# Turning k' over 128 rows and projecting v onto the diagonals of a zeroed bank in a Linformer-attention and SwiGLU kernel

## The chip, the cores and the metric

The kernel runs on one core of one Trainium2 chip. The metric is the device time of one execution in microseconds (us). The **span** of a trace is shorter than that by about 1.7 us (569.4 for an execution of 571.14): it goes from the first to the last instruction.

## The reference

```python
k_proj = einsum('ks,bhsd->bhkd', E, k)              # 8 batches, 8 heads, 1024 tokens, 64 deep
v_proj = einsum('ks,bhsd->bhkd', F, v)              # k and v are shortened to 64 rows a head
attn   = softmax(q @ k_proj.T / 8)                  # 1024 x 64 per head
x      = (attn @ v_proj).transpose(0, 2, 1, 3).reshape(8192, 512)
out    = (silu(x @ w_gate) * (x @ w_val)) @ w_out   # w_gate, w_val 512 x 1536; w_out 1536 x 512
```

Inputs and output are fp32. The kernel computes in bf16 with fp32 sums.

## The kernel before

The gated network takes most of TensorE's time. It goes through 16 chunks of 512 tokens, two a batch, and for each of 12 blocks of 128 features makes one group of four matmuls for the gate (`gps`) and one for the value (`vps`). Two such groups of a block are followed by part of an output (`yps`). Between the groups lie numbered **slots**, in which the attention of the next chunk or batch is placed, piece by piece. Batches are numbered from 0 in the code and here; "second batch" at a timeline near 55 us is batch 1. Batch 0 can hide behind nothing: its attention is the start of the program, and the first two blocks are worked in two token halves, each as soon as its x is there.

The projection of k and v, and the turning of the projected k (k'), before the change:

```python
def u_KV(b, what="kv", hs=(0, H), at="a"):
    ...
    for j in range(NJ):                                  # k to rows 0-63 of the bank, v to rows 64-127
        for _, lo, w, src in todo:
            nc.tensor.matmul(out=t[lo:lo+64, h0:h1]..., lhsT=w[:, j, :], rhs=src[b][:, h0:h1, j, :], ...)
    if "k" in what:                                      # ks has 64 partitions
        nc.scalar.copy(out=kvp[b, "s"][:, h0:h1], in_=t[0:64, h0:h1])
    if "v" in what:                                      # even heads to one diagonal block, odd to the other
        eng = nc.vector if b else nc.scalar
        copy(eng, BDV[b % 2][0:64, ps, 0:64], tv[:, ps, 0, :])
        copy(eng, BDV[b % 2][64:128, ps, 64:128], tv[:, ps, 1, :])

def u_KT(b, at="a", prs=(0, NPAIR)):
    t = bank(at, [P, NPAIR, KP], BF16, "kTp")
    for pr in range(*prs):                               # 64 rows x 128 columns, turned to 128 x 64
        nc.tensor.transpose(out=t[:, pr, :], in_=ks[:, 2*pr:2*pr+2, :]..., identity=ident_bf[:KP, :KP])
    ...                                                  # VectorE copies kTp into the diagonals of BD
```

`BD` and `BDV` hold k' and v' of two heads on the diagonal of a 128x128 tile, so that one matmul serves two heads. The order of the start, after the fourth set of scores:

```python
u_KV(0, "v", (0, 4), at="y"); warm(1); u_KV(0, "v", (4, 6), at="y")
u_PV2(0, 0, 0, 0, act);       u_A(0, 2, dve)             # attention product; turning of attention weights
u_KV(0, "v", (6, 8), at="y"); u_A(0, 1, act)
u_PV2(0, 0, 1, 0, act);       u_A(0, 3, dve);  u_PV2(0, 0, 0, 1, dve)
load_w_gv(4, 6);  load_q(0, 1);  load_w_gv(6, 8) ...     # one queue, in this order
```

Batches 1 to 7 get their transposed q (`qTd`) by a transposing transfer on SyncE's queue (`u_TD`).

The softmax here doesn't subtract the row's maximum and nothing guards it: scores larger than these inputs give would overflow.

## Time and profile before

| what | us | from |
|---|---|---|
| time, median of 3 executions | 571.42 (571.02 to 571.66) | results |
| lost at changes of form, 47.5 us to the end | 3.39, of this 1.53 at k' | starts of TensorE's groups, less their regular spacing |
| TensorE's waits for weights of blocks 6 and 7 | 0.76 | the same |
| TensorE's wait for x of the second chunk | 0.47 | the same |
| slack of batch 2's first transposed q | 0.46 | landing at 104.58, first scores at 105.04 |

The sum of the busy time cannot show the losses at the changes of form. This is the windows view of the kernel before (from:to, length, then busy us and instructions of each engine, granted clock, DMA share in units of one engine's time, GB/s):

```profile
core 0: us, PE busy (x) PEld busy (x) DVE busy (x) ACT busy (x) POOL busy (x), PEclk, DMA share, GB/s
47.50:569.00 521.50, 518.43 (x2637) 241.04 (x2635) 304.32 (x514) 209.97 (x364) 79.47 (x80) 1.00 0.57 103
```

TensorE seems idle for 521.50 - 518.43 = 3.07 us. But an end of a matmul is modelled, and the length that the profile gives a matmul runs on into a drain. The losses are read from starts alone: group start to group start, less the number of matmuls times their spacing (0.216 us for 512 columns, 0.056 for 128, about 0.03 for 64).

### The profile page before, as it was taken

The numbers are of one execution on the slowest core, as the hardware profiler recorded it, in microseconds if no ns is written. First come the engines' busy times: TensorE is split into PE (matmuls) and PEld (weight loads), VectorE is DVE, ScalarE is ACT, GpSimd is POOL, SyncE is SP. The second block draws the span as 40 slices with busy tenths as digits, with TensorE's granted clock in tenths as the row PEclk, the third lists the DMA queues.
The fourth block names the chain that finished last, engine by engine and source line by source line (L and its number), as shares of the span: only waits on it lengthen the run. The fifth ranks groups of instructions, "written<-read, shape, count | busy, mean of one in ns | idle before, by whom it ended". The sixth has DMA issues, their size and how long they took to land.

```text
span 569.4 us, 7879 instructions
## 1 busy us (share of the span) xinstructions
PE 562.6 (99%) x2939; PEld 266.7 (47%) x2939; DVE 335.2 (59%) x577; ACT 236.8 (42%) x417; POOL 109.1 (19%) x122
## 2 busy tenths in 40 slices
PE   8999999999999999999999999999999999999997
PEld 5654444444444444444444444444444444444444
DVE  4776664766476655666466655666546665545550
ACT  4565442454435433443435434354343543443222
POOL 6742250124002400124002230023100220000000
PEclk9999999999999999999999999999999999999999
DMA  9999979829903696039931399105990213010002
GB/s 211 179 199 198 167 131 201 141 60 205 198 18 75 108 177 141 37 56 158 189 79 38 75 178 207 41 20 104 191 185 20 57 38 75 37 38 37 20 37 94
DMA packets 111143, 62.91 MB, mean 110 GB/s; under 512 B 64256, under 2 KB 102400, under 8 KB 111104
## 3 DMA queue, kind: packets, MB, share of 16 engines
q0 software_dynamic: 42800, 29.36, 36.3%
q1 hardware_dynamic: 67392, 31.46, 25.6%
q10 hardware_dynamic: 912, 1.57, 0.9%
q8 instruction: 23, 0.38, 0.3%
q14 instruction: 16, 0.13, 0.1%
HBM read 60.29 MB, written 16.78 MB: 135 GB/s over the span
## 4 chain that ended last, share of the span: by engine, by line
PE 92%; DMA 3%; DVE 2%; POOL 1%; ACT 1%; issue 0%; ACTq 0%; DVEq 0%; POOLq 0%
PE yps L362 29%; PE vps L324 28%; PE gps L324 27%; PE kvp L149 3%; PE sc L229 2%; PE pv L287 2%; DMA wv<-in_moe_w_val_dram 2%; DMA kraw<-in_k_dram 1%; DVE zz L244 1%; POOL AA L260 0%; POOL wg L117 0%; DVE hT L348 0%; ACT xT L137 0%; DVE s L343 0%; PE kTp L174 0%
## 5 line engine op out<-in xcount | busy, mean ns | idle before, releaser
L343 DVE SCALAR_TENSOR_TENSOR s<-th,gps 128x512 f32<-128x512 f32 x192 | 130.5, 679 | 143.1 <-ACT th L336 143.0
L324 PE MATMUL gps<-xT,wg 128*128 128x512 bf16 (+1 forms) x776 | 197.8, 377 | 0.6 <-DMA wg<-in_moe_w_gate_dram 0.4
L324 PE MATMUL vps<-xT,wv 128*128 128x512 bf16 (+1 forms) x776 | 197.5, 377 | 0.1
L362 PE MATMUL yps<-wo,hT 128*128 128x512 bf16 (+1 forms) x780 | 194.5, 376 | 0.0
L336 ACT ACTIVATE th<-gps 128x512 f32<-128x512 f32 x192 | 114.6, 597 | 157.9 <-PE gps L324 156.4
L348 DVE TENSOR_TENSOR hT<-s,vps 128x512 bf16<-128x512 f32 x192 | 132.0, 688 | 20.0
L260 POOL TENSOR_TENSOR AAd<-ee,rr 128x512 bf16<-128x512 f32 x56 | 58.3, 1041 | 343.3 <-issue 157.2
L362 PEld LDWEIGHTS <-hT 128*128 128x128 bf16 x780 | 76.2, 98 | 89.9
L324 PEld LDWEIGHTS <-wv 128*128 128x128 bf16 x776 | 73.9, 98 | 83.9 <-issue 3.3
L324 PEld LDWEIGHTS <-wg 128*128 128x128 bf16 x776 | 73.9, 98 | 82.1 <-issue 1.0
L372 ACT ACTIVATE ysb<-yps 128x512 f32<-128x512 f32 (+1 forms) x65 | 38.4, 591 | 76.7 <-PE yps L362 76.7
L137 ACT CAST xT<-pv 128x512 bf16<-128x512 f32 x63 | 36.6, 585 | 51.0 <-PE pv L287 50.1
L244 DVE TENSOR_REDUCE zz<-ee 128x8 f32<-128x512 f32 x64 | 43.4, 679 | 21.8 <-ACT ee L233 21.8
L233 ACT ACTIVATE ee<-sc 128x512 f32<-128x512 f32 x64 | 37.9, 595 | 23.6 <-PE sc L229 22.3
L229 PEld LDWEIGHTS <-qTd 128*128 128x128 bf16 x224 | 17.2, 98 | 13.2
L287 PE MATMUL pv<-AT,BDV 128*128 128x512 bf16 x60 | 22.4, 379 | 0.0
L229 PE MATMUL sc<-BD,qTd 128*128 128x128 bf16 x224 | 21.6, 219 | 0.0
L137 DVE CAST BDV<-kvp 64x256 bf16<-64x256 f32 x14 | 6.0, 426 | 20.0 <-ACT ks L159 17.8
L246 DVE RECIPROCAL rr<-zz 128x8 f32<-128x8 f32 x64 | 13.0, 203 | 7.4 <-DVE zz L244 1.4
L149 PE MATMUL kvp<-vb,FT 128*64 128x512 bf16 (+2 forms) x80 | 15.6, 338 | 0.3 <-ACT BDV L137 0.3
L149 PE MATMUL kvp<-kb,ET 128*64 128x512 bf16 (+1 forms) x72 | 15.5, 357 | 0.5 <-DMA kb<-in_k_dram 0.3
L107 POOL DMA_DIRECT2D qb<-in_q_dram x17 | 15.6, 919 | 0.6 <-DMA wv<-in_moe_w_val_dram 0.6
(51 smaller groups left out, 126.3 us busy)
## 6 DMA issues: line engine op xcount, KB each, us to landing
out_dram<-ysb SPq DMA_DIRECT2D x63, 256.0 KB, 2.4
qb<-in_q_dram POOLq DMA_DIRECT2D x15, 512.0 KB, 18.2
kb<-in_k_dram POOLq DMA_DIRECT2D x7, 1024.0 KB, 11.0
vb<-in_v_dram POOLq DMA_DIRECT2D x7, 1024.0 KB, 14.4
wo<-in_moe_w_out_dram POOLq DMA_DIRECT2D x2, 768.0 KB, 21.8
wg<-in_moe_w_gate_dram POOLq DMA_DIRECT2D x5, 256.0 KB, 9.5
wv<-in_moe_w_val_dram POOLq DMA_DIRECT2D x5, 256.0 KB, 10.1
kraw<-in_k_dram ACTq DMA_DIRECT2D x2, 512.0 KB, 4.7
```

Of the source, the lines that this page charges most:

```text
L137: (nc.scalar.copy if eng is nc.scalar else eng.tensor_copy)(out=out, in_=in_)
L149: nc.tensor.matmul(out=t[lo : lo + 64, h0:h1].rearrange("p h d -> p (h d)"), lhsT=w[:, j, :], rhs=src[b][:, h0:h1, j, :], start=(j == 0), ...
L229: nc.tensor.matmul(out=ps[:, n, :], lhsT=t[:, n, :], rhs=BD[b % 2][:, 4 * g + n, :], start=True, stop=True)
L233: nc.scalar.activation(out=e[:].rearrange("p h j k -> p (h j k)"), in_=ps[:].rearrange("p a k -> p (a k)"), func=AF.Exp, scale=scale,)
L244: nc.vector.reduce_sum(out=z[:], in_=e[:], axis=AX.X)
L260: eng.tensor_tensor(out=a.rearrange("p j h k -> p h j k"), in0=ee.pop((b, u))[:], in1=rr.pop((b, u))[:].unsqueeze(3).to_broadcast([P, 4, 2 ...
L324: nc.tensor.matmul(out=ps[:, ts], lhsT=(wg, wv)[w][:, kt, f * P : (f + 1) * P], rhs=x[:, kt, ts], start=(kt == 0), stop=(kt == NKT - 1),)
L336: nc.scalar.activation(out=th[:], in_=ps[:], func=AF.Tanh, scale=0.5)
L343: nc.vector.scalar_tensor_tensor(out=s1[:], in0=th[:], scalar=1.0, in1=g[:], op0=ALU.add, op1=ALU.mult)
L348: nc.vector.tensor_tensor(out=hT[c][:, f, :], in0=s1[:], in1=ps[:], op=ALU.mult)
L362: nc.tensor.matmul(out=yy[c][:, cs], lhsT=hT[c][:, f, i * P : (i + 1) * P], rhs=wo[:, f, cs], start=(f == 0), stop=(f == NFT - 1),)
L372: nc.scalar.activation(out=ysb[:, cs], in_=yy[c][:, cs], func=AF.Copy, scale=0.5)
```

## The change

It has four parts. **k'**: turned over all 128 rows (the lower 64 zero), to have the form of the matmuls beside it. **v of the first batch**: projected straight onto the diagonals of a bank that one matmul of zeros has cleared, so that one copy takes a piece out instead of two; the order of the start is rearranged with it. **q of the second chunk**: loaded in head halves, so that the weights of blocks 6 and 7 come ahead of its second half. **Slots**: the second chunk's attention one slot earlier, its last copies on two engines.

```diff
+    ks = [const.tile([P, H, D], BF16, name=f"ks{i}") for i in range(2)]     # rows 64-127 set to 0
...
+            nc.scalar.copy(out=ks[b % 2][0:64, h0:h1], in_=t[0:64, h0:h1])
...
+    def u_V0(p0, p1, at):
+        t = bank(at, [P, p1 - p0, P], FP32, "kvp")
+        nc.tensor.matmul(out=t[:]..., lhsT=zeros[:, 0:P], rhs=zeros[:, 0 : (p1 - p0) * P], start=True, stop=False)
+        src = vb[0][:].rearrange("p (a c) j d -> p a c j d", c=2)
+        for j in range(NJ):
+            for c in range(2):
+                nc.tensor.matmul(
+                    out=t[64 * c : 64 * c + 64, :, 64 * c : 64 * c + 64],
+                    lhsT=FT[:, j, :], rhs=src[:, p0:p1, c, j, :], start=False, stop=(j == NJ - 1))
+        nc.scalar.copy(out=BDV[0][:, p0:p1, :], in_=t[:])
...
-        t = bank(at, [P, NPAIR, KP], BF16, "kTp")
+        t = bank(at, [P, NPAIR, KP], FP32, "kTp")
-            nc.tensor.transpose(out=t[:, pr, :], in_=ks[...], identity=ident_bf[:KP, :KP])
+            nc.tensor.matmul(out=t[:, pr, :], lhsT=ks[b % 2][...], rhs=ident_bf[:, 0:KP], start=True, stop=True)
...
-        for i in range(2): ... nc.vector.memset(BDV[i][:], 0.0)
+        nc.vector.memset(BDV[1][:], 0.0)                                     # and two memsets of ks[i][64:P]
...  (order of the start)
+        u_V0(0, 2, "y");  u_PV2(0, 0, 0, 0, act);  warm(1);  u_V0(2, 3, "y");  u_A(0, 2, dve)
+        u_PV1(0, 0, 2, 0, dve)
+        u_V0(3, 4, "v");  u_PV1(0, 0, 3, 0, act);  u_N(0, 3)
+        f_mm(0, 0, 0, 0); u_A(0, 1, act);  u_A(0, 3, dve);  f_mm(0, 0, 1, 0)
+        u_PV2(0, 0, 0, 1, act);  u_PV2(0, 0, 1, 1, dve);  f_mm(0, 1, 0, 0);  f_mm(0, 1, 1, 0)
...
-        load_q(0, 1)
+        load_q(0, 1, hs=(0, 4));  load_w_gv(6, 8);  load_q(0, 1, hs=(4, 8));  load_w_gv(8, 10) ...
...
-            put(12 + i, u_T, 0, u);  put(14 + i, u_S, 0, u);  ...  put(19 + i, u_A, 0, u, nc.scalar)
+            put(11 + i, u_T, 0, u);  put(13 + i, u_S, 0, u);  ...  put((17, 18, 20, 21)[i], u_A, 0, u, nc.scalar)
-        put(21, u_PV, 0, 1, 0);  put(22, ...);  put(23, u_PV, 0, 1, 2);  put(23, u_PV, 0, 1, 3)
+        put(19, u_PV, 0, 1, 0);  put(20, ...);  put(22, u_PV, 0, 1, 2);  put(22, u_PV, 0, 1, 3, nc.vector)
```

More of the change, by code (lines that the diff above doesn't have):

```diff
@@ L101, in load_v, with load_q @@
             )
-    def load_q(b, ch, js=(0, 4)):
-        if js[0] == 0:
+    def load_q(b, ch, js=(0, 4), hs=(0, H)):
+        if js[0] == 0 and hs[0] == 0:
             qb[b, ch] = q_pool.tile([P, H, 4, D], BF16, name="qb", tag="qb")
-        js = slice(*js)
+        js, hs = slice(*js), slice(*hs)
         nc.gpsimd.dma_start(
-            out=qb[b, ch][:, :, js, :].rearrange("p h j d -> p h (j d)"),
-            in_=q[b].rearrange("h (p c j) d -> p c h j d", c=2, j=4)[:, ch, :, js, :].rearrange(
+            out=qb[b, ch][:, hs, js, :].rearrange("p h j d -> p h (j d)"),
+            in_=q[b, hs].rearrange("h (p c j) d -> p c h j d", c=2, j=4)[:, ch, :, js, :].rearrange(
                 "p h j d -> p h (j d)"
@@ L156, in u_KV @@
         if "k" in what:
-            if (b, "s") not in kvp:
-                kvp[b, "s"] = aw.tile([KP, H, D], BF16, name="ks", tag="ks")
-            nc.scalar.copy(out=kvp[b, "s"][:, h0:h1], in_=t[0:64, h0:h1])
+            nc.scalar.copy(out=ks[b % 2][0:64, h0:h1], in_=t[0:64, h0:h1])
         if "v" in what:
@@ L162, in u_KV @@
             ps = slice(h0 // 2, h1 // 2)
-            eng = nc.vector if b else nc.scalar
-            copy(eng, BDV[b % 2][0:64, ps, 0:64], tv[:, ps, 0, :])
-            copy(eng, BDV[b % 2][64:128, ps, 64:128], tv[:, ps, 1, :])
+            nc.vector.tensor_copy(out=BDV[b % 2][0:64, ps, 0:64], in_=tv[:, ps, 0, :])
+            nc.vector.tensor_copy(out=BDV[b % 2][64:128, ps, 64:128], in_=tv[:, ps, 1, :])
         if h1 == H:
             kvp.pop(key)
+    def u_V0(p0, p1, at):
+        t = bank(at, [P, p1 - p0, P], FP32, "kvp")
+        nc.tensor.matmul(
+            out=t[:].rearrange("p a d -> p (a d)"),
+            lhsT=zeros[:, 0:P], rhs=zeros[:, 0 : (p1 - p0) * P],
+            start=True, stop=False,
+        )
+        src = vb[0][:].rearrange("p (a c) j d -> p a c j d", c=2)
+        for j in range(NJ):
+            for c in range(2):
+                nc.tensor.matmul(
+                    out=t[64 * c : 64 * c + 64, :, 64 * c : 64 * c + 64],
+                    lhsT=FT[:, j, :],
+                    rhs=src[:, p0:p1, c, j, :],
+                    start=False,
+                    stop=(j == NJ - 1),
+                )
+        nc.scalar.copy(out=BDV[0][:, p0:p1, :], in_=t[:])
     def u_KT(b, at="a", prs=(0, NPAIR)):
-        ks = kvp[b, "s"]
-        t = bank(at, [P, NPAIR, KP], BF16, "kTp")
+        t = bank(at, [P, NPAIR, KP], FP32, "kTp")
         for pr in range(*prs):
-            nc.tensor.transpose(
+            nc.tensor.matmul(
                 out=t[:, pr, :],
-                in_=ks[:, 2 * pr : 2 * pr + 2, :].rearrange("p h d -> p (h d)"),
-                identity=ident_bf[:KP, :KP],
+                lhsT=ks[b % 2][:, 2 * pr : 2 * pr + 2, :].rearrange("p h d -> p (h d)"),
+                rhs=ident_bf[:, 0:KP],
+                start=True,
+                stop=True,
             )
@@ L309, in u_PV2, with u_PV1 @@
         copy(eng, xT[b, ch][:, 2 * g : 2 * g + 2, 256 * i : 256 * (i + 1)], ps[:])
+    def u_PV1(b, ch, pr, i, eng):
+        ps = ps_a.tile([P, CW // 2], FP32, name="pv", tag="pa")
+        nc.tensor.matmul(
+            out=ps[:].rearrange("p (j t) -> p j t", t=P),
+            lhsT=BDV[b % 2][:, pr, :],
+            rhs=AT[b, ch][:, 2 * i : 2 * i + 2, pr, :],
+            start=True,
+            stop=True,
+        )
+        copy(eng, xT[b, ch][:, pr, 256 * i : 256 * (i + 1)], ps[:])
     gp = {}
@@ L443 @@
         for i in range(2):
+            nc.vector.memset(ks[i][64:P], 0.0)
             nc.vector.memset(BD[i][:], 0.0)
-            nc.vector.memset(BDV[i][:], 0.0)
+        nc.vector.memset(BDV[1][:], 0.0)
         def turn(which, at, halves=(0, 1)):
@@ L512 @@
         u_R(0, 3)
-        u_N(0, 3)
-        u_KV(0, "v", (0, 4), at="y")
-        warm(1)
-        u_KV(0, "v", (4, 6), at="y")
-        u_PV2(0, 0, 0, 0, act)
-        u_A(0, 2, dve)
-        u_KV(0, "v", (6, 8), at="y")
+        u_V0(0, 2, "y")
+        u_PV2(0, 0, 0, 0, act)
+        warm(1)
+        u_V0(2, 3, "y")
+        u_A(0, 2, dve)
+        u_PV1(0, 0, 2, 0, dve)
+        u_V0(3, 4, "v")
+        u_PV1(0, 0, 3, 0, act)
+        u_N(0, 3)
+        f_mm(0, 0, 0, 0)
         u_A(0, 1, act)
-        u_PV2(0, 0, 1, 0, act)
         u_A(0, 3, dve)
-        u_PV2(0, 0, 0, 1, dve)
-        load_w_gv(4, 6)
-        load_q(0, 1)
-        for f in (6, 8, 10):
-            load_w_gv(f, f + 2)
+        f_mm(0, 0, 1, 0)
+        u_PV2(0, 0, 0, 1, act)
+        u_PV2(0, 0, 1, 1, dve)
+        f_mm(0, 1, 0, 0)
+        f_mm(0, 1, 1, 0)
+        load_w_gv(4, 6)
+        load_q(0, 1, hs=(0, 4))
+        load_w_gv(6, 8)
+        load_q(0, 1, hs=(4, 8))
+        load_w_gv(8, 10)
+        load_w_gv(10, 12)
         load_q(1, 0)
@@ L531 @@
         load_wo(1)
-        f_mm(0, 0, 0, 0)
-        u_PV2(0, 0, 1, 1, act)
-        f_mm(0, 0, 1, 0)
-        f_mm(0, 1, 0, 0)
-        f_mm(0, 1, 1, 0)
-        for i, u in enumerate(range(4, 8)):
-            put(12 + i, u_T, 0, u)
-            put(14 + i, u_S, 0, u)
-            put(15 + i, u_R, 0, u)
-            put(15 + i, u_N, 0, u)
-            put(19 + i, u_A, 0, u, nc.scalar)
-        put(21, u_PV, 0, 1, 0)
-        put(22, u_PV, 0, 1, 1)
-        put(23, u_PV, 0, 1, 2)
-        put(23, u_PV, 0, 1, 3)
+        for i, u in enumerate(range(4, 8)):
+            put(11 + i, u_T, 0, u)
+            put(13 + i, u_S, 0, u)
+            put(14 + i, u_R, 0, u)
+            put(14 + i, u_N, 0, u)
+            put((17, 18, 20, 21)[i], u_A, 0, u, nc.scalar)
+        put(19, u_PV, 0, 1, 0)
+        put(20, u_PV, 0, 1, 1)
+        put(22, u_PV, 0, 1, 2)
+        put(22, u_PV, 0, 1, 3, nc.vector)
         put(20, load_v, 1)
```

## The prediction

> **What bounds the kernel now.** I read the page first, then the chain of waits, then the timeline of TensorE, looking for stretches in which it stands still.
>
> ```profile
> PE 562.6 (99%) x2939; PEld 266.7 (47%) x2939; DVE 335.2 (59%) x577; ACT 236.8 (42%) x417; POOL 109.1 (19%) x122
> ...
> PE 92%; DMA 3%; DVE 2%; POOL 1%; ACT 1%; issue 0%; ACTq 0%; DVEq 0%; POOLq 0%
> ```
>
> TensorE is busy 99% of 569.4 us and makes up 92% of the chain that ends last. All other engines have idle time in plenty. So the change can win only what TensorE loses, and each loss has to be looked up: a matmul of 512 columns starts every 0.216 us when nothing is in the way, a group of four every 0.865 us, and what lies above that is loss. In the steady part (47.5 us to the end) I found no wait of TensorE at all by that count, only this (timeline of TensorE, second batch: start, length, group):
>
> ```profile
> 55.53 1.03 PE L324 MATMUL gps<-xT,wg 128*128 128x512 bf16 x4
> 56.49 0.29 PE L174 MATMUL kTp<-ident_bf,ks 64*128 64x64 bf16 x4
> 56.71 1.04 PE L324 MATMUL vps<-xT,wv 128*128 128x512 bf16 x4
> 57.59 1.03 PE L362 MATMUL yps<-wo,hT 128*128 128x512 bf16 x4
> ```
>
> The group at 55.53 is through at 56.39, the k' transposes (64 rows) start at 56.49, and the four of them, 0.03 apart, would be over at 56.61, but the next group starts at 56.71. So there is about 0.10 us lost going into the 64-row form and 0.10 coming out. Summed over the seven later batches, the steady part loses 3.4 us so, some 1.5 at the k' transposes, the rest at the projections (128*64), which stay. Before 47.5 us there are true waits (timeline, start-up and first chunk):
>
> ```profile
> 16.50 0.39 PE L464 MATMUL warm<-zeros 128*128 128x512 bf16 x1
> 17.19 0.61 PE L149 MATMUL kvp<-vb,FT 128*64 128x128 bf16 x8 [0.30 <-ACT BDV L137]
> ...
> 19.48 0.39 PE L302 MATMUL pv<-AT,BDV 128*128 128x256 bf16 x2 [0.24 <-DVE AT L137]
> 20.04 0.38 PE L276 MATMUL aTp<-ident_bf,AA 128*128 128x128 bf16 x4 [0.17 <-ACT AT L137]
> ...
> 22.46 0.60 PE L324 MATMUL gps<-xT,wg 128*128 128x256 bf16 x4
> ...
> 31.89 1.04 PE L324 MATMUL gps<-xT,wg 128*128 128x512 bf16 x4 [0.35 <-DMA wg<-in_moe_w_gate_dram]
> 32.77 0.39 PE L195 MATMUL qTp<-ident_bf,qb 128*128 128x128 bf16 x4
> 33.21 1.04 PE L324 MATMUL vps<-xT,wv 128*128 128x512 bf16 x4
> ...
> 46.22 1.48 PE L324 MATMUL gps<-xT,wg 128*128 128x512 bf16 x4
> 47.54 1.02 PE L324 MATMUL vps<-xT,wv 128*128 128x512 bf16 x4
> ```
>
> To be seen: v's projection of heads 4-5 waits for the copy of heads 0-3 out of the same bank; from 22.46 the second half of the tokens starts; at 31.89 and 33.21 TensorE waits for weights (0.52 and 0.23 us late by the spacing); at 46.22 the second chunk's first group takes 1.32 us instead of 0.865, because the last xT copies come late (0.47 lost). The chain of waits names the transfer for the second of these:
>
> ```profile
> 23.11 10.06 DMA wv<-in_moe_w_val_dram
> 33.21 1.04 PE vps L324 x4
> ```
>
> **What the Trainium skill says.** (1) "TensorEngine Tiling (Array Packing)", Tiling Modes, Key Properties: changing the tiling mode drains TensorE, while tiles of one mode run in parallel. The trace agrees: 0.10 us at each change of form, none between forms of 128*128; and in the later batches the k and v projections (two 64-column tiles) start 3 ns apart and 16 of 512 columns take 1.85 us, so two run at once. (2) "PSUM — Partial Sum Buffer", The four PSUM rules: a starting matmul clears the written-bits of the whole bank over the quadrants it writes. That is why the new projection zeroes the bank with one matmul of zeros and then only accumulates; no run of before shows it. (3) "VectorE: DVE Perf Modes", Why PSUM operands drop a tier: bf16 out of PSUM keeps a doubled rate, fp32 doesn't. The trace agrees: a 64x256 copy out of k's bf16 bank takes 0.28 us (median), the like copy of v out of fp32 0.43.
>
> **The change, part by part.**
>
> *k' over 128 rows.* Per batch the four transposes keep their 64 moving columns, but are now of the 128*128 form of their neighbours. Removed: 0.098 + 0.095 us of drain, and twice 0.013 of a late follower, 0.22 per batch, seven batches: 1.53 us, all on the engine that sets the end. If loading 128 rows paces them at 0.056 apart instead of 0.033 (the spacing of the 128-column transposes), some 0.6 comes back. I take 1.4. Added: fp32 instead of bf16 in PSUM, so VectorE's four copies take 0.43 instead of 0.28, 0.6 us more a batch beside a busy TensorE: free. In the first batch they lie on the path: 128 columns each, 0.22 to an estimated 0.29 (half of the difference at 256), four in a row are 0.28 more, less 0.1 of drain saved: 0.2 later at the first scores, and 0.3 at the fourth scores, since VectorE has AT and qT to copy behind the second four. The two added memsets of ks end by 3.1 us, before VectorE's first copy at 4.37: free.
>
> *v onto the diagonals.* Pieces are now heads 0-3, 4-5, 6-7, each one zero matmul and 16 projections in pairs of column tiles. A pair costs what one cost: 8 times 0.055 for the first piece (before 8 times 0.108), perhaps 0.04 each for the small ones. One ScalarE copy replaces two: 0.37 instead of 0.54 for the first piece, about 0.26 instead of 0.43 for the others; 0.5 us of ScalarE in all. But the order has become a ladder. TensorE is in order, and pair 3's projection now stands behind pair 2's attention product, which needs its AT copy. By hand, from the fourth scores at 15.47 (before 15.16): first piece 15.7 to 16.4, copied at 17.05, product 17.1, warm, second piece 17.7 to 18.1, AA of unit 2 transposed by 18.45, AT copied at 19.1, pair 2's product 19.1, third piece 19.4 to 19.8, copied at 20.3, product 20.35, xT copied at 21.0; the first gate group, started at 20.4, ends at 21.15; two transposes, first value group to 22.0; AT copies at 22.2, two products, two groups; the second token half starts at 23.4. Before: 22.46. So this part is about 0.95 us **slower** up to there, 0.3 of it from the fp32 copies.
>
> *q in head halves.* The transfers on that queue land one after another, about 1.3 us for each half MB of fp32 read. Half of q (0.5 MB) goes behind the weights that TensorE waits for, so wg and wv of blocks 6-7 land 1.3 us earlier (33.17 to about 31.8), and TensorE comes 0.95 later: the 0.52, 0.23 and 0.01 of waits are gone, 0.76 us. q's second half lands when wv did, near 33.2, and is needed two slots after the first (block 6's gate and value groups, 0.865 each, and a transpose), near 34.5: in time, with 1.3 us to spare.
>
> *The moved slots.* Transposes, scores and products of the second chunk come one slot earlier, and the last two xT copies are spread over two engines, with a value group of 0.865 us between them and their reader. The 0.47 us at 46.22 should go. Against it: two AT units have one slot less between GpSimd's product and their transpose; I allow 0.15 of new waits.
>
> Sum: -1.4 + 0.95 - 0.76 - 0.47 + 0.15 = -1.53. From 571.42 that is **569.9 us**.
>
> **Rivals.** (a) *The start eats it all.* If the ladder costs more, say 1.5 us, or q's second half lands late, the first chunk ends where it did or later: 570.5 to 571. For it: three in-order hand-overs between TensorE, ScalarE and VectorE where before there were two. Against: half of that delay is waiting that the weights forced anyway. (b) *The start is no slower.* ScalarE's shorter copies and the paired projections might win more than the ladder loses; then 568.8 to 569. For it: ScalarE is copying most of the time there. Against: in my working ScalarE waits for TensorE at the third piece, not the other way. (c) *k' is paced by its weight loads*, or needs the drain for another reason than its row count: then 0.6 to 1.5 us of the gain is missing, 570.5 to 571.4. (d) *A hidden transfer comes forward*: the transposed q of the second batch lands at 61.07 and is first used at 61.90; with TensorE more than 0.8 us ahead it would begin to wait there. I expect it 0.6 ahead.
>
> **Range and chances.** Each term is a few tenths of a us unsure, the start most (0.6). Together about 1 us either way, and the three runs of before spread 0.6: 568.7 to 571.3 for 8 in 10. 2% is 11.4 us; no wait in the trace is a tenth of that, and TensorE's work is the same. So within 2% is nearly sure: 0.98, with 0.01 on either side.
>
> **What would show it.** Right: at the later k' groups TensorE's next group starts about 0.12 us after the first k' transpose is due, not 0.32; VectorE's BD copies take 0.43; no wait on wg or wv near 32; the second chunk's first gate group takes 1.03; the first group of the second token half starts near 23.4. Wrong: it starts before 22.5 (then the ladder isn't one) or after 24; a new wait of a qTp transpose for qb near 33, of aTp for AA near 39 to 43, or of sc for qTd near 61. The prediction falls if the steady part still loses 3 us to changes of form, or if a stage before 47 us loses over 1 us anew.

## The result, and the profile after

The changed kernel took **570.06 us** (median of six executions, 569.53 to 570.79); the kernel before took 571.47 in the same rounds (571.02 to 571.66). The ratio is 0.9978, with a 95% interval of 0.9965 to 0.9991: a real gain of a quarter of a per cent. Here and below a ratio is the mean time of one kernel's fast executions over that of the other's in the same rounds, so not quite the ratio of the medians.

The profiled execution of the changed kernel took 570.49 us, one of its slower ones, so its span is only 0.7 us below that of before. Its page, engines and chain of waits:

```profile
PE 560.7 (99%) x2966; PEld 266.4 (47%) x2966; DVE 340.3 (60%) x580; ACT 235.5 (41%) x413; POOL 109.8 (19%) x123
...
PE 95%; DMA 3%; ACT 1%; DVE 0%; POOL 0%; issue 0%; POOLq 0%
```

TensorE has 27 instructions more and is still the bound; VectorE has all but left the chain. The windows view of the steady part:

```profile
core 0: us, PE busy (x) PEld busy (x) DVE busy (x) ACT busy (x) POOL busy (x), PEclk, DMA share, GB/s
47.50:568.00 520.50, 517.39 (x2639) 241.28 (x2636) 308.55 (x516) 210.01 (x364) 79.46 (x80) 1.00 0.58 103
```

TensorE's apparent idle time is 3.11 us, no smaller than before. What has gone left the busy column, as said above. The starts show it; the timeline of TensorE after, second batch (start, length, group):

```profile
55.79 1.03 PE L358 MATMUL gps<-xT,wg 128*128 128x512 bf16 x4
56.65 0.28 PE L194 MATMUL kTp<-ident_bf,ks 128*128 128x64 bf16 x4
56.77 1.03 PE L358 MATMUL vps<-xT,wv 128*128 128x512 bf16 x4
57.63 1.03 PE L396 MATMUL yps<-wo,hT 128*128 128x512 bf16 x4
```

The gate group takes its regular 0.86 us, the four k' matmuls take 0.12 and the value group follows at once: 0.98 us from 55.79 to 56.77, where before it was 1.18. Over the steady part the loss fell from 3.39 to 2.43 us. Of the 2.43, 1.87 is what the projections lose, which kept their form, and 0.56 is a new wait (below).

The fourth scores of the first batch, TensorE before:

```profile
15.16 0.40 PE L229 MATMUL sc<-BD,qT 128*128 128x128 bf16 x4 [0.18 <-DVE qT L137]
```

The timeline of TensorE after, start and first chunk:

```profile
8.40 1.03 PE L150 MATMUL kvp<-kb,ET 128*64 128x256 bf16 x8
...
16.04 0.40 PE L251 MATMUL sc<-BD,qT 128*128 128x128 bf16 x4 [0.18 <-DVE qT L138]
...
19.46 0.27 PE L336 MATMUL pv<-AT,BDV 128*128 128x256 bf16 x1 [0.52 <-DVE AT L138]
...
20.52 0.28 PE L336 MATMUL pv<-AT,BDV 128*128 128x256 bf16 x1 [0.36 <-ACT BDV L185]
...
23.74 0.60 PE L358 MATMUL gps<-xT,wg 128*128 128x256 bf16 x4
...
32.88 1.03 PE L358 MATMUL gps<-xT,wg 128*128 128x512 bf16 x4
...
33.96 1.03 PE L358 MATMUL vps<-xT,wv 128*128 128x512 bf16 x4
...
46.93 1.03 PE L358 MATMUL gps<-xT,wg 128*128 128x512 bf16 x4
47.79 1.03 PE L358 MATMUL vps<-xT,wv 128*128 128x512 bf16 x4
```

The two products at 19.46 and 20.52 wait for the copy of attention weights and for the copy of v': these are the rungs of the ladder. The second token half starts at 23.74 instead of 22.46. From the fourth scores to there it is 7.70 us (23.74 - 16.04), where before it was 7.30 (22.46 - 15.16). The groups at 32.88 and 33.96 no longer wait for weights, and the group at 46.93 takes its regular 0.86 us. But already the first k projection starts at 8.40, 0.54 us later than the 7.86 of before, which nothing in the prediction accounts for.

Farther on, a wait has come that was not there. The timeline of TensorE near 105 us in the kernel before, then after:

```profile
104.18 1.03 PE L362 MATMUL yps<-wo,hT 128*128 128x512 bf16 x4
105.04 0.39 PE L229 MATMUL sc<-BD,qTd 128*128 128x128 bf16 x4
```

```profile
104.01 1.03 PE L396 MATMUL yps<-wo,hT 128*128 128x512 bf16 x4
105.43 0.40 PE L251 MATMUL sc<-BD,qTd 128*128 128x128 bf16 x4 [0.39 <-DMA qTd<-qb]
```

These are batch 2's first scores. TensorE comes 0.17 us earlier than before, and stands: 105.43 - 104.01 is 1.42 us, 0.56 above the regular spacing (the bracket counts from the modelled end of the last matmul). The chain of waits names the transfer (start, length):

```profile
98.59 6.80 DMA qTd<-qb
```

The transposed q, issued at 98.59, landed at 105.39; before, issued at 98.49, it landed at 104.58. So TensorE's 0.17 us would not have used up the slack of 0.46. The wait comes mainly from the transfer, which took 6.80 us from issue to landing instead of 6.09.

| difference of the two spans, us | |
|---|---|
| first k projection later | +0.54 |
| from there to the second token half | +0.74 |
| weights' waits gone (0.52 and 0.22 at the two larger ones) | -0.73 |
| wait for the second chunk's x gone | -0.46 |
| aTp's wait gone at 42 (0.15); new waits of a qTp transpose for q (0.12) and of the first product for attention weights (0.24) | +0.21 |
| k' drains gone | -1.52 |
| new wait for batch 2's transposed q | +0.56 |
| sum | -0.66 |

The spans differ by 0.7. In the rounds the means differ by 1.27 us (571.41 and 570.14): the profiled execution of the changed kernel (570.49) was 0.35 slower than its mean, that of the kernel before (571.14) 0.27 faster than its mean.

### The profile page after: what moved, and what is told of

Read it like the earlier page. It is cut to its first block, busy times and chain, and to the rows that moved or that the text cites. A ratio compares the mean times of both kernels' runs of the same rounds, so it can differ in the third digit from the quotient of the medians.

```text
span 568.7 us, 7931 instructions
## 1 busy us (share of the span) xinstructions
PE 560.7 (99%) x2966; PEld 266.4 (47%) x2966; DVE 340.3 (60%) x580; ACT 235.5 (41%) x413; POOL 109.8 (19%) x123
## 4 chain that ended last, share of the span: by engine, by line
PE 95%; DMA 3%; ACT 1%; DVE 0%; POOL 0%; issue 0%; POOLq 0%
PE gps L358 29%; PE yps L396 29%; PE vps L358 29%; PE kvp L150 3%; PE sc L251 2%; PE pv L309 2%; DMA qb<-in_q_dram 1%; DMA qTd<-qb 1%; PE aTp L298 0%; PE qTp L217 0%; ACT ee L255 0%; ACT th L370 0%; POOL AA L282 0%; PE pv L324 0%; PE kTp L194 0%
## 5 line engine op out<-in xcount | busy, mean ns | idle before, releaser
L138 ACT CAST xT<-pv 128x512 bf16<-128x512 f32 (+1 forms) x62 | 35.9, 581 | 51.8 <-PE pv L309 50.5
L162 DVE CAST BDV<-kvp 64x256 bf16<-64x256 f32 x7 | 3.0, 426 | 20.0 <-ACT ks L158 17.8
L150 PE MATMUL kvp<-vb,FT 128*64 128x512 bf16 x56 | 13.4, 382 | 0.0
```

The costliest lines, as they stand in the source:

```text
L138: (nc.scalar.copy if eng is nc.scalar else eng.tensor_copy)(out=out, in_=in_)
L150: nc.tensor.matmul(out=t[lo : lo + 64, h0:h1].rearrange("p h d -> p (h d)"), lhsT=w[:, j, :], rhs=src[b][:, h0:h1, j, :], start=(j == 0), ...
```

## The experiments

Twelve runs were made in three calls, each beside the kernel before; those of one call share a chip. The kernel before had means of 571.41 us in the rounds of the result and 571.37, 571.39 and 571.36 in the three calls, so means are compared across calls too, with care. All gave the right result. "2nd - k1" is the time from the first k projection to the first gate group of the second token half, from the trace; it takes the start of k out of the comparison. A few traces lack some records of matmuls (a group marked x3 or a hole of one spacing); such holes are not counted as waits.

| run | median (range), us | ratio to before, 95% interval | span | 2nd - k1 |
|---|---|---|---|---|
| after_again | 570.09 (569.55-570.81) | 0.9980 (0.9967-0.9992) | 569.0 | 15.47 |
| v_swap | 569.97 (569.50-570.93) | 0.9978 (0.9964-0.9992) | 569.0 | 14.76 |
| v_old | 569.06 (568.82-570.76) | 0.9968 (0.9955-0.9980) | 567.3 | 14.77 |
| s_later | 569.59 (569.43-570.05) | 0.9972 (0.9960-0.9985) | 568.0 | 15.28 |
| k_only | 570.34 (569.73-570.95) | 0.9982 (0.9969-0.9994) | 569.2 | 14.99 |
| k64 | 571.24 (570.96-572.05) | 1.0000 (0.9987-1.0012) | 569.4 | 15.39 |
| q_whole | 570.71 (570.40-571.48) | 0.9991 (0.9978-1.0005) | 568.9 | 15.43 |
| slots_old | 570.60 (570.10-570.99) | 0.9985 (0.9972-0.9997) | 568.9 | 15.31 |
| before_again | 571.44 (one execution) | none | 569.6 | 14.74 |
| best_swap | 569.75 (569.10-569.78) | 0.9969 (0.9955-0.9983) | 567.9 | 14.71 |
| best_old | 569.06 (568.78-569.37) | 0.9960 (0.9947-0.9973) | 567.0 | 14.73 |
| best_k0 | 568.65 (568.65-569.30) | 0.9955 (0.9942-0.9968) | 566.9 | 14.72 |

### First call: the start, and the wait at 105 us

**after_again** is the changed kernel once more, unedited.

> The changed kernel once more, unaltered, as the yardstick of this call. All theories: 1.2 to 1.6 us below the kernel before. In its trace the second token half of the first chunk should start 23.2 to 23.7 us from the start. Whether the first scores of the second batch (near 105 us) wait for the transposed q again (0.56 us in the first trace) decides between two readings: if that wait is of the change, it is there again; if it is luck of one transfer, it is smaller or gone.

It repeats the result, and in its trace the late start too (first k projection at 8.69, second token half at 24.16) and the wait for batch 2's transposed q (0.52). These belong to the kernel and not to one odd execution. The token half is later than the 23.2 to 23.7 expected here, and past the 24 that the prediction had named as a sign of being wrong.

**v_swap** moves one line: pair 3's projection goes ahead of pair 2's product, so that it no longer stands behind the copy of the attention weights.

```diff
-        u_PV1(0, 0, 2, 0, dve)
         u_V0(3, 4, "v")
+        u_PV1(0, 0, 2, 0, dve)
```

> The changed kernel with one line moved: the third piece of v is projected before pair 2's attention product instead of after it. Theory (the start became a ladder of in-order hand-overs): TensorE's wait of about 0.5 us between the third projection and pair 3's product shrinks, and the second token half starts 0.5 to 0.7 us earlier than in the unaltered changed kernel; the time falls by 0.3 to 0.7 us. Rival (the start is set by the DMA of v's last heads or by GpSimd's AA): TensorE waits for vb or AA instead, and the start moves by less than 0.2 us.

Timeline of TensorE, v_swap:

```profile
23.23 0.60 PE L358 MATMUL gps<-xT,wg 128*128 128x256 bf16 x4
...
34.31 0.39 PE L251 MATMUL sc<-BD,qT 128*128 128x128 bf16 x4
34.77 0.40 PE L217 MATMUL qTp<-ident_bf,qb 128*128 128x128 bf16 x4
...
103.73 1.03 PE L396 MATMUL yps<-wo,hT 128*128 128x512 bf16 x4
105.69 0.40 PE L251 MATMUL sc<-BD,qTd 128*128 128x128 bf16 x4 [0.93 <-DMA qTd<-qb]
```

The second token half starts at 23.23, and 2nd - k1 falls from 15.34 or 15.47 to 14.76, hardly more than the 14.60 and 14.74 of the kernel before. Counted from the fourth scores, which leaves out what is ahead of the ladder, the traces fall into three groups: 7.28 to 7.30 us in the six with v as before, 7.70 to 7.71 in the six with the new order, 7.02 and 6.99 in v_swap and best_swap. So the ladder is the order of two lines, worth 0.7 us in the trace, and with the lines swapped the new v projection is 0.3 faster there than the old one.

**The time doesn't move** (569.97 against 570.09), where 0.3 to 0.7 us less was expected. TensorE arrives earlier at three transfers and waits there: 0.23 us for the second half of the second chunk's q (the transpose at 34.77; the transfer landed at 34.72), where after_again waited 0.06; 0.12 us at 61.65 for batch 1's transposed q (landed at 61.61), where after_again did not wait; and 1.10 us at 105 us (105.69 - 103.73 - 0.86), where after_again waited 0.52. That is 0.87 of the 0.93 us by which the second token half came earlier than in after_again (23.23 against 24.16).

**v_old** takes the new v part out and keeps the rest: v projected, copied and ordered as before (both halves of `u_KV`'s copies, the memset of both BDV, the old order of the start).

```diff
-        u_V0(0, 2, "y")
-        u_PV2(0, 0, 0, 0, act)
+        u_N(0, 3)
+        u_KV(0, "v", (0, 4), at="y")
         warm(1)
-        u_V0(2, 3, "y")
+        u_KV(0, "v", (4, 6), at="y")
+        u_PV2(0, 0, 0, 0, act)
         ...                                  # and so on, as in the kernel before
```

> The changed kernel with v projected, copied and ordered as in the kernel before; k' over 128 rows, q in halves and the moved slots stay. Theory (the v part costs about 0.7 us at the start): the second token half starts 0.5 to 0.9 us earlier than in the unaltered changed kernel, and the time is 0.4 to 0.8 us lower. Rival (the v part is a gain, and the late start comes from the fp32 copies of k' and from the landing of k): it starts as late or later, and the time is the same or higher.

It is about 0.7 us faster than the changed kernel in the mean (569.42, against 570.14 of the changed kernel's eleven executions; one of its five took 570.76). The intervals overlap; the clean comparison comes with best_old below, which is s_later with this same edit: its slowest execution (569.37) is faster than the fastest of s_later (569.43, another call on the same chip). The new v part, then, doesn't pay. In this trace the transposed q of batch 2 was issued at 97.70 and landed at 103.8, before its reader, so that nothing was lost there: TensorE was earlier, but so was the transfer's issue, and it took 6.10 us.

**s_later** leaves everything and puts batch 2's scores one slot later.

```diff
-            o = 13 if b == 2 else 6
+            o = 14 if b == 2 else 6
```

> The changed kernel with the second batch's scores one slot later. Theory (TensorE, being earlier, runs into the transposed q of the second batch): the wait near 105 us is gone, and if the unaltered kernel shows it in most executions the time falls by about 0.5 us. Rival (that wait was luck of the one traced execution): the time is within 0.2 us of the unaltered one.

The trace has no wait for the transposed q (the scores start at 105.63, 0.86 us after the gate group at 104.77). The mean is 569.69, 0.45 below the changed kernel's, and the range shrinks from 1.3 us to 0.6. The intervals overlap, so the time alone wouldn't prove it; with the trace it fits a wait that the changed kernel has in most of its executions.

### Second call: the parts alone

**k_only** is the kernel before with the k' part alone: the 128-row `ks`, its memsets and copy, and the fp32 matmul.

```diff
+            nc.scalar.copy(out=ks[b % 2][0:64, h0:h1], in_=t[0:64, h0:h1])
-        t = bank(at, [P, NPAIR, KP], BF16, "kTp")
+        t = bank(at, [P, NPAIR, KP], FP32, "kTp")
-            nc.tensor.transpose(...)
+            nc.tensor.matmul(out=t[:, pr, :], lhsT=ks[b % 2][...], rhs=ident_bf[:, 0:KP], ...)
```

> The kernel before with the k' part alone (ks of 128 rows, zeroed once; matmul against the identity; fp32 in PSUM). Theory (two drains of 0.10 us per batch are gone): no loss at the k' groups in the trace, 1.4 to 1.5 us less lost there from 47 us on; at the start the second token half begins 0.2 to 0.4 us later, mostly absorbed by the wait for weights near 32 us; the time is 1.0 to 1.5 us below the kernel before. Rival (TensorE gains nothing because it meets the transposed q near 105 us or other waits): those waits appear and the time is less than 0.6 us below.

The gaps at k' are gone from all seven later batches, and the mean gain is 1.0 us of the 1.5 that they were worth. The second token half starts 0.25 to 0.39 us later, counted from the first k projection, as was expected of the fp32 copies. Where the rest can go is in the trace of its profiled execution. Timeline of TensorE, k_only:

```profile
33.16 1.04 PE L324 MATMUL gps<-xT,wg 128*128 128x512 bf16 x4 [1.23 <-DMA wg<-in_moe_w_gate_dram]
...
34.54 1.04 PE L324 MATMUL vps<-xT,wv 128*128 128x512 bf16 x4
```

It waits 1.40 us for the weights of blocks 6 and 7 at the first group and 0.28 at the second, against 0.52 and 0.23 in the kernel before. The issue order is that of before. In the trace a transfer has landed when the last of its 16 reports is in: the first report of this weight transfer came at 31.01, as before (30.99), and the last at 33.12 instead of 31.85. This lag, 0.7 to 2.1 us for this transfer over the fourteen traces, differs from execution to execution.

**k64** is the changed kernel with k' turned over 64 rows, but still as a matmul into fp32: of the k' part only the number of rows is undone.

```diff
-                lhsT=ks[b % 2][:, 2 * pr : 2 * pr + 2, :]...,     rhs=ident_bf[:, 0:KP],
+                lhsT=ks[b % 2][0:KP, 2 * pr : 2 * pr + 2, :]...,  rhs=ident_bf[0:KP, 0:KP],
```

> The changed kernel with the k' matmul over 64 rows again, still a matmul and still fp32 in PSUM. Theory (the row count is what makes TensorE drain): two gaps of 0.10 us per batch at k' are back, 1.5 us in all, and the time is about 1.0 to 1.5 us above the changed kernel, that is within 0.5 of the kernel before. Rival (it was the transpose mode or the 2-byte output): no gaps, and the time is that of the changed kernel.

Timeline of TensorE, k64, second batch:

```profile
55.62 1.03 PE L358 MATMUL gps<-xT,wg 128*128 128x512 bf16 x4
56.58 0.29 PE L194 MATMUL kTp<-ident_bf,ks 64*128 64x64 bf16 x4
56.80 1.04 PE L358 MATMUL vps<-xT,wv 128*128 128x512 bf16 x4
```

From 55.62 to 56.80 is 1.18 us, as in the kernel before, and so it is in all seven batches: about 0.098 going in and 0.096 coming out. The mean is 571.37, 1.23 above the changed kernel's eleven executions. It is the row count that does it, not the operation or the type in PSUM, and it is worth almost the whole gain of the change. (The two were timed in different calls.)

**q_whole** loads the second chunk's q whole, ahead of the weights of blocks 6 and 7, and keeps the rest of the change.

```diff
-        load_q(0, 1, hs=(0, 4))
+        load_q(0, 1)
         load_w_gv(6, 8)
-        load_q(0, 1, hs=(4, 8))
```

> The changed kernel with the second chunk's q in one transfer ahead of the weights of blocks 6 and 7. Theory of the prediction (the split takes 0.76 us of waits away): TensorE waits 0.4 us or more for wg or wv near 33 us, and the time is 0.3 to 0.8 us higher. Rival (the later start alone already lets those weights land in time): waits for weights of 0.3 us at most, the 0.1 us wait of a q transpose near 35 us gone, and the time the same within 0.2 us.

Its mean (570.85) is 0.7 above that of the changed kernel, which was timed in another call (the means of before were 571.39 and 571.37 to 571.41 there). Its trace shows only one wait for these weights, 0.22 us, as the rival of the expectation had it, while the time is what the theory had. The trace of the one execution does not show where the 0.7 comes from. The lag just described is a likely cause, since with q ahead of the weights every longer lag meets TensorE, but that is argued, not shown.

**slots_old** keeps all but the moved slots: the table of the second chunk is that of before.

```diff
-            put(11 + i, u_T, 0, u) ... put((17, 18, 20, 21)[i], u_A, 0, u, nc.scalar)
+            put(12 + i, u_T, 0, u) ... put(19 + i, u_A, 0, u, nc.scalar)
-        put(19, u_PV, 0, 1, 0) ... put(22, u_PV, 0, 1, 3, nc.vector)
+        put(21, u_PV, 0, 1, 0) ... put(23, u_PV, 0, 1, 3)
```

> The changed kernel with the second chunk's transposes, scores and products in the slots of the kernel before. Theory (the earlier slots and the split between two engines take 0.47 us of waiting for xT away): the first gate group of the second chunk again loses 0.4 to 0.5 us, the 0.24 us before the first product near 42 us is gone, and the time is 0.2 to 0.3 us higher. Rival (the wait for xT came from the start or from the weights and is gone anyway): no loss there, and the time is 0.2 us lower.

Timeline of TensorE, slots_old:

```profile
46.64 1.48 PE L358 MATMUL gps<-xT,wg 128*128 128x512 bf16 x4
47.96 1.02 PE L358 MATMUL vps<-xT,wv 128*128 128x512 bf16 x4
```

The group takes 1.32 us again, as in the kernel before: the 0.47 is back, so the moved slots are what removed it. The mean is 570.51, 0.37 above the changed kernel's, as the net of the table above would have it (0.46 and 0.15 gone, 0.24 new); but the executions overlap and the calls differ, so it is the trace that shows it.

### Third call: a better version

**before_again** is the kernel before, unedited, for a second trace.

> The kernel before, traced a second time. If the waits for the weights of blocks 6 and 7 near 32 us (0.75 us in its first trace, 1.68 in that of the kernel with the k' part alone) are set by how far the slowest of the 16 DMA engines lags, they differ here from 0.75 although nothing has changed; if they are fixed by the order of the transfers, they are 0.75 again within 0.1. The landing of the second k transfer, 7.0 us in all traces with v projected as before and 7.4 to 7.7 in all with the new projection, should be near 7.0 if that pattern is more than chance.

Its landmarks repeat those of the first trace: first k projection at 7.86, second token half at 22.60, 0.47 lost at the second chunk's x. Its waits for weights are 0.61 and 0.28, together 0.15 more than in the first trace: they do vary with nothing changed, but much less than up to k_only's 1.68.

**best_swap** is v_swap with `o = 14`, **best_old** is v_old with `o = 14`, and **best_k0** is best_old with the first batch's k' turned over 64 rows into bf16, as before.

```diff
-        t = bank(at, [P, NPAIR, KP], FP32, "kTp")
+        t = bank(at, [P, NPAIR, KP], FP32 if b else BF16, "kTp")
         for pr in range(*prs):
+            if b == 0:
+                nc.tensor.transpose(out=t[:, pr, :], in_=ks[0][0:KP, ...], identity=ident_bf[:KP, :KP])
+                continue
```

> The changed kernel with the third v piece ahead of pair 2's product and the second batch's scores one slot later. Theory (the ladder cost 0.6 us at the start, which the wait for the transposed q near 105 us took back): now both are gone, the time is 568.8 to 569.4 us, 0.6 to 1.1 below the changed kernel. Rival (the start is not on the path): the time is that of the changed kernel with the later scores alone, about 1.8 us below the kernel before.

> v as in the kernel before, with k' over 128 rows, q in halves, the moved slots, and the second batch's scores one slot later. Theory (the new v projection gains nothing once its ladder is gone): within 0.3 us of the kernel with the swapped line and later scores. Rival (its shorter copies do count): that one is 0.4 us or more faster.

> The kernel of the run ahead of it, but the first batch's k' is transposed over 64 rows into 2-byte PSUM as before; later batches stay at 128 rows. Theory (the fp32 copies of BD cost 0.3 to 0.4 us on the start's path): BD copies of 128 columns take 0.22 us instead of 0.28 to 0.29, the fourth scores of the first batch start 0.2 to 0.4 us earlier, and the time is 0.2 to 0.4 us lower, the lowest of all. Rival (that delay is hidden by later waits): the time is the same within 0.15 us.

best_swap gains nothing over s_later (569.75 against 569.59) and misses the 568.8 to 569.4 expected. The swap's 0.6 us are there (14.71), the wait at 105 us is gone, and TensorE now waits for the second half of the second chunk's q instead, 0.54 us by the spacing. Timeline of TensorE, best_swap:

```profile
34.93 0.40 PE L217 MATMUL qTp<-ident_bf,qb 128*128 128x128 bf16 x4 [0.37 <-DMA qb<-in_q_dram]
```

best_old is 0.5 us faster than best_swap in the mean (569.08 against 569.61; the ranges overlap), not within 0.3 as expected. It has neither wait, and its span is 0.9 us below best_swap's: 0.54 of this is that wait, and 0.39 the earlier first k projection (7.99 against 8.38). best_k0 is the fastest of all, 0.9955 of the kernel before, and **beats both kernels**: its slowest execution took 569.30, the fastest of the changed kernel's eleven 569.53. Whether the first batch's bf16 copies are worth anything on top of best_old is not settled. The medians differ by 0.4 us and the intervals overlap. Timelines of best_k0:

```profile
9.91 0.22 DVE L212 COPY BD<-kTp 64x128 bf16<-64x128 bf16 x1 [2.07 <-PE kTp L196]
...
22.61 0.60 PE L366 MATMUL gps<-xT,wg 128*128 128x256 bf16 x4
```

The first four BD copies take 0.95 us from start to end here (1.21 in best_old), but 2nd - k1 is 14.72 against 14.73: in this trace q's first transfer landed later, and took the gain away.

### What stays open

The first k projection waits for the second of k's two first transfers. It landed at 6.99 to 7.08 us in the six traces in which v is projected as before (the two of before, k_only, v_old, best_old, best_k0), and at 7.36 to 7.73 in the eight with the new projection. The k projection began at 7.86 to 8.11 and at 8.32 to 8.69. Fourteen traces fall apart without overlap, so the programs with the new v projection start about 0.45 us later there. It is not that transfer alone: E landed at 5.41 to 5.70 and at 5.93 to 6.11. And batch 2's first transposed q, far from the start, took 6.09 to 6.23 us from issue to landing in the same six traces and 6.47 to 6.97 in the same eight; this is most of what brought the wait at 105 us. Yet up to 7 us the two sorts of program differ in nothing that I can name but one memset of BDV fewer on VectorE. No run changed that alone. The effect is shown; its cause is not.

## Why the prediction was right or wrong

The time was 570.06 where 569.9 was predicted, and within 2% of before. Step by step:

- **k' drains: right.** 1.5 us are gone, and k64 shows that the row count alone did it. Its rival, k' paced by its weight loads, fell: the next group starts 0.12 us after the first of the four, as the first check of the prediction asked. The fp32 BD copies came out as estimated. These are the tile views of BD, before and after (count, shortest/median/longest in ns, first and last start, forms):

```profile
L182 DVE COPY BD<-kTp x18: 216/275/293, 9.7 to 432.6; 64x256 bf16<-64x256 bf16 x14, 64x128 bf16<-64x128 bf16 x4
```

```profile
L204 DVE CAST BD<-kTp x18: 282/409/427, 10.4 to 432.5; 64x256 bf16<-64x256 f32 x14, 64x128 bf16<-64x128 f32 x4
```

  The estimate was 0.29 for 128 columns; the four of the first batch are the shortest, from 0.28. Four in a row cost 0.26 us more (1.21 against 0.95). From the first k projection to the fourth scores the two traces of before took 7.30 and 7.45 and best_k0 7.44, the eleven with fp32 copies 7.45 to 7.77, in the mean 0.25 more; the prediction had 0.3. The execution times alone do not show it.
- **The start ladder: the mechanism was right, its size was not.** The prediction gave 0.95 in all, 0.63 of it from the fourth scores to the second token half (23.4 less 15.47, against 7.30) and 0.3 for the copies ahead of them. From the fourth scores it measured 0.40 (7.70 against 7.30), and v_swap turns this into a gain of 0.28. The landmark (23.4 predicted, 23.74 found, 24.16 in after_again) was passed because of the later landing of k, a term that the sum did not have (0.54 in the traced pair).
- **Weights: right in the trace.** The waits for blocks 6 and 7 are gone. wg and wv were issued 0.74 and 0.72 us later than before and landed 0.56 and 0.50 earlier, so the split of q is worth the 1.3 us that the prediction gave it. But the prediction put the whole saving down to the split. With the split undone, the later start alone hides most of the waits in the trace (0.22 left). In the mean of the executions, undoing the split costs 0.7 us, so it seems to pay, though the intervals overlap and the two were timed in different calls. The second half of q was not in time with 1.3 us to spare: of its 16 reports the first came at 32.98, the last at 35.13 instead of 33.2.
- **The moved slots: right.** 0.46 is gone, and slots_old brings it back. The new wait at the attention weights is 0.24, not 0.15, but an old one of 0.15 went, so net it was near the prediction. The wait of a qTp transpose for q, 0.12, was named among the things that could go wrong; it came, from that late last report, and it is what v_swap (0.23) and best_swap (0.54) ran into.
- **The hidden transfer (rival d): right in kind, wrong in place.** The prediction looked for it at 61 us, with batch 1's transposed q, and took the steady part for free of it. It came at 105 us, with batch 2's, which had 0.46 us of slack before. In most traces of the changed kernel and its near kin it costs about 0.5, with v_swap 1.1. (At 61 us it came too in two traces: 0.12 in v_swap, 0.08 in v_old.) This is the step that failed: the check of slack covered one reader of such a transfer instead of every one, and it took the transfer's time as fixed, while this one took 6.80 us instead of 6.09.

In the traced pair the sum was not right: it came to -0.66 instead of -1.53. Not foreseen were 0.54 at k's landing and 0.56 at 105 us, against a start smaller by 0.2 and k' drains larger by 0.1. The mean of the executions fell by 1.27, much nearer, because the changed kernel was profiled in a slower execution than its mean and the kernel before in a faster one. That the time came within 0.2 us of the prediction is therefore partly luck, since two terms of half a microsecond were missing from it. With the 0.66 of the traced pair it would have been 570.8, still within 568.7 to 571.3.

## What to carry to other kernels

Where TensorE is 99% busy, look for losses in the starts of its groups rather than in its idle time: a group of matmuls with 64 rows among ones with 128 cost 0.2 us each time, and filling its rows with zeros took that cost away. Before moving work earlier, list every transfer whose reader comes close behind its landing, because a TensorE that is ahead by half a microsecond may only wait half a microsecond longer at the next one; v_swap and best_swap did just that. And do not take a landing as fixed: the wait at 105 us came more from a transfer that took 0.7 us longer than from an earlier TensorE. In a start-up where engines hand to one another in turn, the order of two lines can be worth more than the instructions saved: the order cost 0.7 us, while the new projection itself, with its one copy less a piece, won 0.3 there with the better order, and the kernels with the old projection were still 0.5 to 0.7 us faster in the mean.

## What the Trainium skill lacked or had wrong

- "TensorEngine Tiling (Array Packing)", Tiling Modes, Key Properties, says that changing the mode drains TensorE, but not what it costs. Here it was 0.098 us going into a group of 64 rows and 0.096 coming out, in each of seven batches, so filling the rows with zeros pays.
- "TensorE: Matmul & The Clock Gate", Back-to-back issue gap, gives some 81 ns at 128 columns and 131 ns at 512 for sustained pairs of load and matmul, and keeps its formula, N / 2.4 + 2.5 ns for N columns, for isolated matmuls. These traces, with a weight load for every matmul and TensorE 99% busy, show 56 ns and 216 ns throughout, which is the formula. (An earlier part of the same page has 55.6 and 215.7 ns for matmuls back to back, so the page is at odds with itself.)
- "DMA: Bandwidth & Descriptors", Latency and other measured facts, says that two of the 16 DMA engines are usually slower. It gives no size. Here the last of 16 reports of the weight transfer of blocks 6 and 7 came 0.7 to 2.1 us after the first and varied between executions; which engine it was, the trace doesn't tell.
- No page that I found says how long a transposing transfer within SBUF takes beside other traffic; the pages give only rates. Here the 512 KB of transposed q (128x2048, bf16) took 4.2 to 8.5 us from issue to landing over the fourteen traces, and 18 to 19 us for batch 1's first, which was issued near 42 us; batch 2's first took 6.1 to 7.0.
